# Sliding-window attention with a leaky-ReLU feed-forward behind it: first layer by halves of 288 tokens, rings for its operands, attention steps placed by matmul time, output tiles copied and issued by ACT

## Chip, cores, metric

One core of one Trainium2 chip. The metric is the time of one launch on the device in microseconds, median of several runs. Engines: PE does matmuls, DVE and ACT elementwise work (both reach the matmul result banks), POOL elementwise work in SBUF, SP only issues transfers.

## The reference

```python
# q, k, v: 8 batches x 8 heads x 576 tokens x 64, float32; window 32
scores = (q @ k.T) / 8;  mask = abs(i - j) <= 32
attn = softmax(where(mask, scores, -1e9));  y = attn @ v
x = y.transpose(0, 2, 1, 3).reshape(4608, 512)
h = x @ w_in                      # 512 -> 2048
g = maximum(0.01 * h, h)
out = g @ w_out                   # 2048 -> 512, float32
```

## The kernel before

The attention of one half batch (288 queries) and one pair of heads is a *step*; four steps make the 288 tokens of a half ready, 64 steps are done in all. A step is: `score` of the next step (five matmuls into `ps`, `exp` on ACT into `e`, mask on POOL into `pr`) and `weighted` of this one:

```python
def weighted(i):
    ...
    x = xps.tile([128, HALF], FP32, name="x")      # one bank each
    s = xps.tile([128, HALF], FP32, name="s")
    nc.tensor.matmul(s, ones_bd, pr[:, 0:HALF], ...)          # 2 matmuls: row sums
    ...                                                       # 5 matmuls into x
    r = attn.tile([128, HALF], FP32, name="r")
    nc.vector.reciprocal(r, s)
    t0 = b * S + hf * HALF
    nc.vector.tensor_mul(xT[:, p, t0:t0 + HALF], x, r)
```

The feed-forward works in groups of 256 or 384 tokens. `h_tile` makes 128 rows of the first layer in one of three banks (`mm`), and ACT empties it; `o_tile` makes 128 tokens of output in one of the same three banks:

```python
def h_tile(t0, n, f):
    h = mmps.tile([128, 512], FP32, name="mm", tag="mm")
    for c in range(DMC):                                      # 4 matmuls of n columns
        nc.tensor.matmul(h[:, 0:n], w_in_bf[:, c, ts(f, 128)], xT[:, c, ds(t0, n)], ...)
    nc.scalar.activation(out=gT[t0][:, f, 0:n], in_=h[:, 0:n], func=AF.Prelu, alpha=0.01)

def o_tile(t0, j, midway=None):
    o = mmps.tile([128, 512], FP32, name="mm", tag="mm")
    for f in range(FFC):                                      # 16 matmuls of 512 columns
        nc.tensor.matmul(o, gT[t0][:, f, ts(j, 128)], w_out_bf[:, f, :], ...)
        ...
    o_sb = outp.tile([128, DMODEL], FP32, name="o_sb")
    nc.vector.tensor_copy(out=o_sb, in_=o)
    nc.sync.dma_start(out=out[ds(t0 + j * 128, 128), :], in_=o_sb)
```

Transposes of q and k (`tp`, one bank, emptied by ACT into `qT` and `kT`; DVE copies `kT` into `kbd`) come one group of six with most steps. Where the steps stand is decided by pieces (a third or half of a group's first layer, or one output tile), not by time:

```python
groups = [(512 + 256 * i, 256) for i in range(3)]
groups += [(1280 + 384 * i, 384) for i in range(8)] + [(1280 + 384 * 8, 256)]
...                                                           # groups -> pieces ("chunks")
for ci, (_, kind, t0, n, a, m) in enumerate(chunks):
    goal = base + -(-(NC - base) * (ci + 1) // span)
    for cj in range(ci, len(chunks)):
        lead = 1 if cj < 12 else 2
        goal = max(goal, chunks[cj][0] - int(RATE * max(cj - lead - ci, 0)))
    while state["done"] < min(goal, NC):
        step()                                                # one, two or none
    ...
```

A group of 384 tokens does not match halves of 288: some groups need one new half, others two.

The softmax here doesn't subtract the row's maximum and nothing guards it: scores larger than these inputs give would overflow.

## Time and profile before

| | busy, us | share |
|---|---|---|
| PE matmul | 324.3 | 92% |
| DVE | 211.8 | 60% |
| ACT | 183.4 | 52% |
| POOL | 178.7 | 51% |
| span of the profiled run | 353.9 | |
| time, median | 356.09 | |

PE is busy nearly all the time, so the question is where it is not. The view of what PE waited for tells who held it, but its times are shorter than the loss, since a matmul's record runs on for about 0.17 us after the next could have started. To size a loss, the prediction and this document take the distance between the starts of two matmuls and subtract the distance usual for that pair.

What PE waited for between 50 and 320 us, kernel before, the three longest lines of five (engine, line, releaser: us in total, times, longest):

```profile
PE s L238 <- DVE r L252: 3.8, 5, 1.2
PE tp L187 <- ACT qT L195: 2.2, 3, 0.7
PE x L246 <- POOL vbd L175: 1.0, 2, 0.6
```

The first two are attention steps and transposes that stood too close behind another; the third is a step that came before POOL had cast its v (`vbd`).

### The profile page before, as it was taken

The numbers are of one execution on the slowest core, as the hardware profiler recorded it, in microseconds if no ns is written. First come the engines' busy times: TensorE is split into PE (matmuls) and PEld (weight loads), VectorE is DVE, ScalarE is ACT, GpSimd is POOL, SyncE is SP. The second block draws the span as 40 slices with busy tenths as digits, with TensorE's granted clock in tenths as the row PEclk, the third lists the DMA queues.
The fourth block names the chain that finished last, engine by engine and source line by source line (L and its number), as shares of the span: only waits on it lengthen the run. The fifth ranks groups of instructions, "written<-read, shape, count | busy, mean of one in ns | idle before, by whom it ended". The sixth has DMA issues, their size and how long they took to land.

```text
span 353.9 us, 6635 instructions
## 1 busy us (share of the span) xinstructions
PE 324.3 (92%) x2600; PEld 208.2 (59%) x2624; DVE 211.8 (60%) x242; ACT 183.4 (52%) x363; POOL 178.7 (51%) x213
## 2 busy tenths in 40 slices
PE   2658998999989898999999898999999999999995
PEld 1437864584957655656656555656656656555472
DVE  5588647757686877645653778554676676630101
ACT  5765862292845637518527527716528517326060
POOL 7797676578765766524543568533655423200000
PEclk9999999999999999999999999999999999999999
DMA  8999986599995274342453265340010010020101
GB/s 187 214 205 236 269 162 182 144 201 235 209 255 146 58 222 133 69 126 88 140 162 70 63 177 165 88 124 33 0 61 30 2 61 31 5 86 0 61 31 59
DMA packets 60707, 42.37 MB, mean 120 GB/s; under 512 B 39684, under 2 KB 56068, under 8 KB 60676
## 3 DMA queue, kind: packets, MB, share of 16 engines
q1 hardware_dynamic: 56388, 37.76, 42.7%
q0 software_dynamic: 4288, 4.20, 7.2%
q8 instruction: 20, 0.33, 0.4%
q14 instruction: 11, 0.09, 0.1%
HBM read 36.70 MB, written 9.44 MB: 130 GB/s over the span
## 4 chain that ended last, share of the span: by engine, by line
PE 77%; DMA 7%; DVE 6%; POOL 4%; SPq 2%; issue 2%; ACT 1%; DVEq 0%; POOLq 0%; ACTq 0%
PE mm L273 33%; PE mm L264 31%; DMA kf<-in_k_dram 7%; DVE r L252 5%; PE x L246 3%; PE tp L187 3%; PE ps L220 3%; PE s L238 2%; PE s L239 2%; SPq L71 1%; POOL vbd L175 1%; POOL vbd L400 1%; SPq L82 1%; DVE xT L254 1%; POOL pr L230 1%
## 5 line engine op out<-in xcount | busy, mean ns | idle before, releaser
L252 DVE RECIPROCAL r<-s 128x288 f32<-128x288 f32 x64 | 125.1, 1954 | 38.5 <-PE s L239 38.2
L230 POOL TENSOR_TENSOR pr<-e,mask 128x544 bf16<-128x544 bf16 x64 | 77.7, 1213 | 115.0 <-ACT e L226 114.7
L264 PE MATMUL mm<-xT,w_in_bf 128*128 128x384 bf16 (+1 forms) x896 | 132.7, 304 | 0.9 <-ACT kT L201 0.8
L268 ACT ACTIVATE gT<-mm 128x384 bf16<-128x384 f32 (+1 forms) x224 | 99.0, 445 | 63.0 <-PE mm L264 58.6
L273 PE MATMUL mm<-w_out_bf,gT 128*128 128x512 bf16 x552 | 126.8, 379 | 1.3
L264 PEld LDWEIGHTS <-w_in_bf 128*128 128x128 bf16 x896 | 86.6, 98 | 38.0 <-issue 1.3
L273 PEld LDWEIGHTS <-gT 128*128 128x128 bf16 x576 | 54.9, 98 | 61.1
L226 ACT ACTIVATE e<-ps 128x544 bf16<-128x544 f32 x64 | 39.8, 622 | 77.6 <-PE ps L220 77.6
L280 DVE COPY o_sb<-mm 128x512 f32<-128x512 f32 x36 | 24.9, 691 | 66.8 <-PE mm L273 66.8
L204 DVE COPY kbd<-kT 64x576 bf16<-64x576 bf16 x64 | 28.4, 444 | 18.2 <-ACT kT L201 17.6
L175 POOL CAST vbd<-vf 64x576 bf16<-64x576 f32 x58 | 38.3, 661 | 1.9
L254 DVE TENSOR_TENSOR xT<-x,r 128x288 bf16<-128x288 f32 x64 | 29.3, 458 | 7.0 <-PE mm L264 0.5
L165 POOL CAST kb<-kf 96x768 bf16<-96x768 f32 x32 | 26.6, 834 | 9.5 <-DMA kf<-in_k_dram 9.5
L246 PE MATMUL x<-pr,vbd 128*128 128x128 bf16 (+2 forms) x320 | 26.9, 217 | 2.0 <-POOL vbd L175 1.0
L220 PE MATMUL ps<-qT,kbd 128*128 128x128 bf16 (+2 forms) x320 | 27.3, 219 | 0.3
L238 PE MATMUL s<-pr,ones_bd 128*128 128x288 bf16 x64 | 19.0, 297 | 8.7 <-DVE r L252 7.0
L220 PEld LDWEIGHTS <-kbd 128*128 128x128 bf16 x320 | 21.1, 102 | 8.1 <-issue 0.6
L195 ACT ACTIVATE qT<-tp 128x576 bf16<-128x576 bf16 x32 | 20.8, 649 | 9.6 <-PE tp L187 9.0
L246 PEld LDWEIGHTS <-vbd 128*128 128x128 bf16 x320 | 21.4, 101 | 7.1 <-issue 2.8
L201 ACT ACTIVATE kT<-tp 128x576 bf16<-128x576 bf16 x32 | 20.8, 650 | 8.9 <-PE tp L187 7.9
L187 PE MATMUL tp<-ident,qb 96*128 96x96 bf16 x192 | 14.4, 214 | 8.5 <-DVE qb L165 6.7
L165 POOL CAST qb<-qf 96x768 bf16<-96x768 f32 x24 | 19.7, 820 | 0.0
(31 smaller groups left out, 107.7 us busy)
## 6 DMA issues: line engine op xcount, KB each, us to landing
qf<-in_q_dram SPq DMA_DIRECT2D x32, 288.0 KB, 3.5
kf<-in_k_dram SPq DMA_DIRECT2D x32, 288.0 KB, 3.9
vf<-in_v_dram SPq DMA_DIRECT2D x64, 144.0 KB, 3.4
out_dram<-o_sb SPq DMA_DIRECT2D x36, 256.0 KB, 2.2
w_in_bf<-in_moe_w_in_dram POOLq DMA_DIRECT2D x8, 256.0 KB, 6.4
w_out_bf<-in_moe_w_out_dram POOLq DMA_DIRECT2D x4, 512.0 KB, 13.5
qf<-w_in_bf SPq DMA_DIRECT2D x1, 0.0 KB
vf<-w_out_bf SPq DMA_DIRECT2D x1, 0.0 KB
```

The costliest lines, as they stand in the source:

```text
L165: eng.tensor_copy(out=dst[:, p], in_=src[b, p].rearrange("p a (c d) -> p c a d", d=D),)
L175: nc.gpsimd.tensor_copy(out=vbd[b % 2][r, p, :, r], in_=vf[b, p][r])
L204: nc.vector.tensor_copy(out=kbd[b % 2][r, p, :, r], in_=kT[r].rearrange("p (n j) -> p n j", j=64),)
L220: nc.tensor.matmul(ps[:, c0:c0 + n], kbd[b % 2][:, p, blk], qT[b][:, p, q0:q0 + n], start=True, stop=True,)
L226: nc.scalar.activation(out=e, in_=ps[:, 512 - HALF:512 - HALF + NCOL], func=AF.Exp, scale=scale,)
L230: nc.gpsimd.tensor_mul(pr, e, mask[hf])
L246: nc.tensor.matmul(x[:, a:a + n], vbd[b % 2][:, p, blk, :], pr[:, c0:c0 + n], start=(n_ == 0), stop=(n_ == len(WIN[hf]) - 1), skip_group_c ...
L252: nc.vector.reciprocal(r, s)
L254: nc.vector.tensor_mul(xT[:, p, t0:t0 + HALF], x, r)
L264: nc.tensor.matmul(h[:, 0:n], w_in_bf[:, c, ts(f, 128)], xT[:, c, ds(t0, n)], start=(c == 0), stop=(c == DMC - 1),)
L268: nc.scalar.activation(out=gT[t0][:, f, 0:n], in_=h[:, 0:n], func=AF.Prelu, alpha=0.01)
L273: nc.tensor.matmul(o, gT[t0][:, f, ts(j, 128)], w_out_bf[:, f, :], start=(f == 0), stop=(f == FFC - 1),)
```

## The change

The intent, read from the diff: make the unit of the feed-forward the same 288 tokens that attention delivers, so that each unit needs just four steps; hold only four such units of `xT` and `gT`; space the steps evenly by the PE time of what stands between; and take the output tiles off DVE, whose reciprocal PE waited for. Cut to its core:

```diff
-    outp = ctx.enter_context(tc.tile_pool(name="outp", bufs=2))
+    outp = ctx.enter_context(tc.tile_pool(name="outp", bufs=4))
-    xT = const.tile([128, NPAIR, NTOK], BF16)
+    RING = 4 * HALF
+    xT = const.tile([128, NPAIR, RING], BF16)
+    gT = const.tile([128, FFC, RING], BF16)
-    def h_tile(t0, n, f):
+    def h_tile(g, f):
+        t0 = g * HALF % RING
 ...                                        # n columns -> HALF (288) columns
         for f in range(FFC):
+            if hook and f % 4 == 0:
+                hook()
 ...
-        nc.vector.tensor_copy(out=o_sb, in_=o)
-        nc.sync.dma_start(out=out[ds(t0 + j * 128, 128), :], in_=o_sb)
+        nc.scalar.activation(out=o_sb, in_=o, func=AF.Copy)
+        nc.scalar.dma_start(out=out[ts(j, 128), :], in_=o_sb)
 ...                                        # after the first 576 tokens of the first layer:
+    for p in range(NPAIR):
+        load_qk(2, p)                      # was: one after each of the first output tiles
+    H_US, O_US, LEAD = 4 * (HALF / 2400 + 2.5e-3), 4 * 0.216, 4.0
 ...                                        # plan: h_tiles of half g, then the o_tiles it allows
+    for i in range(8, NC):
+        prev = 0.9 * O_US * 4 if i < 12 else at[i // 4 - 1] - LEAD
+        due.append(prev + (at[i // 4] - LEAD + (1.2 if i < 12 else 0) - prev) * (i % 4 + 1) / 4)
+    def spend(us):
+        while due and due[0] <= clock:
+            due.pop(0)
 ...
+            step()
+        clock += us
-    groups = ...; chunks = ...; RATE = 1.3; ...
```

More of the change, by code (lines that the diff above doesn't have):

```diff
@@ L50 @@
     attn = ctx.enter_context(tc.tile_pool(name="attn", bufs=2))
-    moe = ctx.enter_context(tc.tile_pool(name="moe", bufs=2))
-    outp = ctx.enter_context(tc.tile_pool(name="outp", bufs=2))
+    outp = ctx.enter_context(tc.tile_pool(name="outp", bufs=4))
     PS = bass.MemoryType.PSUM
@@ L252, in weighted @@
         nc.vector.reciprocal(r, s)
-        t0 = b * S + hf * HALF
+        t0 = (b * S + hf * HALF) % RING
         nc.vector.tensor_mul(xT[:, p, t0:t0 + HALF], x, r)
-    gT = {}
-    def h_tile(t0, n, f):
-        if f == 0:
-            gT[t0] = moe.tile([128, FFC, 512], BF16, name="gT")
+    gT = const.tile([128, FFC, RING], BF16)
+    def h_tile(g, f):
+        t0 = g * HALF % RING
         h = mmps.tile([128, 512], FP32, name="mm", tag="mm")
@@ L264, in h_tile, with o_tile @@
             nc.tensor.matmul(
-                h[:, 0:n], w_in_bf[:, c, ts(f, 128)], xT[:, c, ds(t0, n)],
+                h[:, 0:HALF], w_in_bf[:, c, ts(f, 128)], xT[:, c, ds(t0, HALF)],
                 start=(c == 0), stop=(c == DMC - 1),
             )
-        nc.scalar.activation(out=gT[t0][:, f, 0:n], in_=h[:, 0:n], func=AF.Prelu, alpha=0.01)
-    def o_tile(t0, j, midway=None):
+        nc.scalar.activation(
+            out=gT[:, f, ds(t0, HALF)], in_=h[:, 0:HALF], func=AF.Prelu, alpha=0.01,
+        )
+    def o_tile(j, hook=None):
         o = mmps.tile([128, 512], FP32, name="mm", tag="mm")
         for f in range(FFC):
+            if hook and f % 4 == 0:
+                hook()
             nc.tensor.matmul(
-                o, gT[t0][:, f, ts(j, 128)], w_out_bf[:, f, :],
+                o, gT[:, f, ds(128 * j % RING, 128)], w_out_bf[:, f, :],
                 start=(f == 0), stop=(f == FFC - 1),
             )
-            if midway and f == FFC // 2 - 1:
-                midway()
         o_sb = outp.tile([128, DMODEL], FP32, name="o_sb")
-        nc.vector.tensor_copy(out=o_sb, in_=o)
-        nc.sync.dma_start(out=out[ds(t0 + j * 128, 128), :], in_=o_sb)
+        nc.scalar.activation(out=o_sb, in_=o, func=AF.Copy)
+        nc.scalar.dma_start(out=out[ts(j, 128), :], in_=o_sb)
     NC = 2 * NPAIR * B
@@ L384 @@
     for f in range(FFC):
-        h_tile(0, 256, f)
+        h_tile(0, f)
         if f in (2, 6, 10):
@@ L395 @@
     for f in range(FFC):
-        h_tile(256, 256, f)
+        h_tile(1, f)
         if f % 4 == 3:
@@ L403 @@
     for p in range(NPAIR):
-        if p < 3:
-            cast_v(1, p)
-            if p == 2:
-                cast_v(1, 3)
-            o_tile(256 * (p // 2), p % 2, step if p == 2 else None)
-            step()
-        else:
-            o_tile(256, 1)
-        load_qk(2, p)
-    for p in range(NPAIR):
-        load_v(2, p)
-    groups = [(512 + 256 * i, 256) for i in range(3)]
-    groups += [(1280 + 384 * i, 384) for i in range(8)] + [(1280 + 384 * 8, 256)]
-    chunks = []
-    for g, (t0, n) in enumerate(groups):
-        need = 4 * -(-(t0 + n) // HALF)
-        nj = n // 128
-        for j in range(nj):
-            f = FFC * j // nj
-            chunks.append((need, "h", t0, n, f, FFC * (j + 1) // nj - f))
-        for j in range(nj):
-            chunks.append((need, "o", t0, n, j, 1))
@@ L429 @@
-    RATE = 1.3
-    base = state["done"]
-    span = len(chunks) - 10
-    for ci, (_, kind, t0, n, a, m) in enumerate(chunks):
-        goal = base + -(-(NC - base) * (ci + 1) // span)
-        for cj in range(ci, len(chunks)):
-            lead = 1 if cj < 12 else 2
-            goal = max(goal, chunks[cj][0] - int(RATE * max(cj - lead - ci, 0)))
-        while state["done"] < min(goal, NC):
-            step()
+        load_qk(2, p)
+    H_US, O_US, LEAD = 4 * (HALF / 2400 + 2.5e-3), 4 * 0.216, 4.0
@@ new lines @@
+    plan = []
+    tiles = 0
+    for g in range(1, 2 * B):
+        if g > 1:
+            plan += [(H_US, "h", g, f) for f in range(FFC)]
+        while 128 * (tiles + 1) <= HALF * (g + 1):
+            plan += [(O_US, "o", tiles, i) for i in range(4)]
+            tiles += 1
+    at, t = {}, 0.0
+    for us, kind, g, f in plan:
+        if kind == "h" and f == 0:
+            at[g] = t
+        t += us
+    due = []
+    for i in range(8, NC):
+        prev = 0.9 * O_US * 4 if i < 12 else at[i // 4 - 1] - LEAD
+        due.append(prev + (at[i // 4] - LEAD + (1.2 if i < 12 else 0) - prev) * (i % 4 + 1) / 4)
@@ L439 @@
+    clock = 0.0
+    cast_v(1, 0)
+    load_v(2, 0)
+    def spend(us):
+        nonlocal clock
+        while due and due[0] <= clock:
+            due.pop(0)
+            i = state["done"]
+            if i < 11:
+                cast_v(1, i - 7)
+                load_v(2, i - 7)
+            step()
+        clock += us
+    for us, kind, g, f in plan:
         if kind == "h":
-            for f in range(a, a + m):
-                h_tile(t0, n, f)
-        else:
-            o_tile(t0, a)
+            spend(us)
+            h_tile(g, f)
+        elif f == 0:
+            o_tile(g, lambda: spend(O_US))
```

## The prediction

> **What bounds the kernel now.** I read the page first (shares, slices, groups), then the waits of PE by stretch, then the timeline of PE, then the timelines of ACT and of the DMA queue around the places where PE stood still.
>
> ```profile
> PE 324.3 (92%) x2600; PEld 208.2 (59%) x2624; DVE 211.8 (60%) x242; ACT 183.4 (52%) x363; POOL 178.7 (51%) x213
> PE   2658998999989898999999898999999999999995
> ...
> L252 DVE RECIPROCAL r<-s 128x288 f32<-128x288 f32 x64 | 125.1, 1954 | 38.5 <-PE s L239 38.2
> ...
> L280 DVE COPY o_sb<-mm 128x512 f32<-128x512 f32 x36 | 24.9, 691 | 66.8 <-PE mm L273 66.8
> ...
> L254 DVE TENSOR_TENSOR xT<-x,r 128x288 bf16<-128x288 f32 x64 | 29.3, 458 | 7.0 <-PE mm L264 0.5
> ```
>
> PE bounds the kernel from about 28 us to 350 us: its digits are 8 or 9 there, no other engine passes 60%. So only two things can gain time: less PE work, or fewer places where PE stands still. The first 28 us (loads, first transposes, first attention steps) are not touched by the diff. The timeline shows where PE stands still:
>
> ```profile
> 101.98 0.29 PE L238 MATMUL s<-pr,ones_bd 128*128 128x288 bf16 x1
> 102.10 0.27 PE L239 MATMUL s<-pr,ones_bd 128*128 128x256 bf16 x1
> 102.21 0.40 PE L246 MATMUL x<-pr,vbd 128*128 128x96 bf16 x5
> 102.45 0.42 PE L187 MATMUL tp<-ident,qb 96*128 96x96 bf16 x6
> 102.91 0.40 PE L220 MATMUL ps<-qT,kbd 128*128 128x64 bf16 x5
> 104.55 0.30 PE L238 MATMUL s<-pr,ones_bd 128*128 128x288 bf16 x1 [1.24 <-DVE r L252]
> ...
> 118.99 0.42 PE L187 MATMUL tp<-ident,qb 96*128 96x96 bf16 x6
> 120.15 0.41 PE L187 MATMUL tp<-ident,kb 96*128 96x96 bf16 x6 [0.74 <-ACT qT L195]
> ```
>
> An attention step (ps, s, x) takes 0.71 us of PE (ps to s 0.24, s to x 0.23, x 0.24) and a transpose group 0.25. At 102 us two steps stand side by side. The second needs the bank of s, which DVE frees only after the reciprocal; so PE loses 1.40 us (ps to s took 1.64, not 0.24), and another 0.32 at x. DVE began that reciprocal late, because it was copying out an output tile, as the chain in order of time says:
>
> ```profile
> 99.96 1.96 PE mm L273 x9
> 101.92 0.02 issue
> 101.94 0.69 DVE o_sb L280
> 102.63 1.88 DVE r L252
> ```
>
> At 119 us two transpose groups stand side by side and the second waits for ACT to empty the one bank: 0.90 us.
>
> I went through the distances from one matmul's start to the next after 28 us, and set aside those of exactly one matmul more, which are records missing from the trace (24 of L273 are missing, 552 of 576). Lost time, over the usual distance: about 3.3 us from 28 to 50, 2.0 from 50 to 70, 1.5 from 70 to 100, 9.3 from 100 to 300, none later; 16 in all. Of the 9.3, four double steps or late steps (102, 135, 202, 216) and two double transposes (119, 200) make nearly all.
>
> **What the Trainium skill says.** "TensorE: Matmul & The Clock Gate", section "Wait — 56ns, not 53.3ns?": warm matmuls follow each other every N ÷ 2.4 GHz plus about 2.5 ns. The trace agrees: 20 matmuls of 384 columns from 158.01 to 161.26, 162.5 ns each (160 + 2.5); 32 of 256 columns in 3.49 us, 109 ns (106.7 + 2.5). "ScalarE: Activation LUTs", section "What ACT_TABLE_LOAD costs": an ACTIVATE with immediate operands takes 186 ns + 0.833 per column, and two in a row overlap by 93. The trace agrees within 20 ns: 490 for 384 columns (506), 384 for 256 (399); at 161.47 a gT of 0.49 was followed at 161.85. "DMA: Bandwidth & Descriptors", section "Issuing engines are not separate DMA queues": issuing from another engine changes only whose sequencer spends the issue time. The trace has that time for SP alone, not for ACT:
>
> ```profile
> L281 SPq DMA_DIRECT2D out_dram<-o_sb x36: 332/362/869, 54.1 to 350.8; - x36
> ```
>
> **The change, part by part.**
>
> *Size of the feed-forward pieces.* The first layer goes from 384 matmuls of 256 columns and 512 of 384 to 1024 of 288. Work: before 384 × 0.109 + 512 × 0.1625 = 125.1 us; after 1024 × 0.1225 = 125.4. So +0.3. The second layer (576 × 0.216 = 124.4) and attention are the same. ACT goes from 224 gT (99.0 us) to 256 of about 411 ns (interpolated between 384 and 490): 105 us.
>
> *Rings.* Only memory: four halves of xT and gT. A slot is rewritten when its readers are three halves, some 60 us, past. I expect no wait from it.
>
> *Even steps.* The instruction order of the changed kernel shows no two steps side by side any more; between two steps stand at least 12 second-layer matmuls (2.6 us) or 28 first-layer ones (3.4), apart from two gaps of 8 (1.7) near 60 us. The step needs DVE for 1.95 + 0.46 = 2.4 us, with the kbd copies (2 × 0.44) 3.3 at most, so s and x come free in time. Double transposes stand once (after a piece of 8 first-layer matmuls, near 88 us), as before. So the 9.3 us from 100 to 300 should go.
>
> *28 to 50 us.* Two waits for DVE (0.32, 0.24) go, since 16 matmuls take 1.96 us in place of 1.75. The last load of k for the second batch lands at 46.7 whatever PE does (PE lost 0.9 there); the larger pieces put 128 × 13.5 ns = 1.7 us more work ahead of it. Most of that is absorbed: gain about 1.5 us. *50 to 70 us.* The first step now comes after 24 second-layer matmuls (5.2 us) in place of 16, which is when POOL has the casts of v ready (52.7 to 55.4): gain 1.6 of 2.0.
>
> *Output tiles from ACT.* DVE is rid of 36 × 0.69 = 25 us. ACT gets 36 copies of 128x512; 490 + 128 × 0.83 = about 597 ns: 21 us; and 36 issues of about 0.36 us, with the hand-over about 0.45: 16 us. In sum ACT goes to about 183 + 6 + 21 = 210 us busy, plus 16 of issuing: 64% of the time, no bound on the whole. Locally it is one. The order "16 second-layer matmuls, step, transpose, 28 first-layer matmuls" occurs 8 times with a transpose. Take the end of the 16 as 0. ACT sees the bank 0.21 later (158.01 to 158.22 in DVE's case), copies until 0.81, issues until about 1.27, then e (0.53 to the next), then qT or kT (0.56), and starts the first gT at 2.37, done at 2.78. PE has finished step and transpose at 0.96 and fills its three banks, one of them that of the output tile, by 2.43. The fourth piece wants the bank of the first gT: PE waits about 0.45. Eight times: 3.6 us. From 70 to 100 us, where a transpose stands close to another, qT now comes after the copy and the issue: two waits grow by 0.8 and 0.5, so this stretch is worse by 1.3.
>
> *End.* The last copy takes 0.60 in place of 0.69, the landing about 2 us as before: −0.1.
>
> Sum: 356.2 − 1.5 − 1.6 + 1.3 − 9.3 + 3.6 + 0.3 − 0.1 = **348.9**, so 349.
>
> **Rivals.** *(a) ACT becomes the bound at every turn from one layer to the other.* For it: issues on SP took up to 0.87 us, and a load of v 3.3 us at 88.6, when the queue was full. If issues on ACT took 0.9 rather than 0.36, each of the 8 waits would be 1.0 us and those with only a step before 28 first-layer matmuls would come in: 8 us in place of 3.6, and about 354. Also, an issue on ACT waits for an earlier transfer that used the same semaphore, often a load on SP; by the order it lies some three steps (13 us) back, but near 57 us it is a load of k that lands only about then. Against it: after 125 us the DMA digits are 2 to 4 and most issues took 0.36. *(b) ACT is not felt at all*, since three banks and 20% slack in the first layer (0.33 against 0.49 us) swallow it. For it: the wait I find is only 0.45. Then 345. *(c) The early stage is bound by transfers and POOL anyway* and gives nothing back: all loads of q and k for the third batch are now issued at once and compete with v. Then the 3.1 us of gain before 70 us fall away: 352. For it: DMA digits of 9 around 45 us, 230 GB/s; against it: those loads queue behind v on one issuer.
>
> **Range and chances.** The limits come from adding rivals: (b) alone 345, (a) alone 354, both of the smaller doubts about ±2. I take 345.5 to 353.5. The line for 2% lies at 349.1, at my point, so chances are even: faster 0.50, within 2% 0.48, slower 0.02 (it would need ACT stalls of over 1 us at all 36 tiles).
>
> **What would show it.** Right: in the PE waits after 100 us no s waiting for r and no kb transpose waiting for qT; the first layer at 1024 matmuls; ACT near 210 us, DVE near 187; a new wait of PE mm for ACT gT, 0.3 to 0.5 us each, about 8 times. Wrong: waits of first-layer matmuls for gT of over 1 us, ACT issues over 0.6 us, s waiting for pr from POOL (e held up on ACT behind an issue), or losses of over 3 us between 50 and 100 us.

## The result

| | before | after |
|---|---|---|
| time, median (4 runs each) | 356.09 us | 350.93 us (350.80 to 351.50) |
| ratio, 95% interval | | 0.9852 (0.9830 to 0.9874) |
| span of the profiled run | 353.9 | 349.3 |
| PE, DVE, ACT, POOL busy | 324.3, 211.8, 183.4, 178.7 | 324.9, 189.2, 203.8, 179.1 |

A ratio here and below is the mean time of one kernel's fast runs over that of the other's fast runs of the same rounds, so not quite the ratio of the medians quoted. The gain is 1.5%: clear of noise, under 2%.

Page of the changed kernel, shares and groups (as in the prediction's first fence: line, engine, operation, shapes, count, then busy us, mean ns, idle before and its releaser):

```profile
PE 324.9 (93%) x2731; PEld 221.3 (63%) x2752; DVE 189.2 (54%) x206; ACT 203.8 (58%) x431; POOL 179.1 (51%) x213
...
L266 PE MATMUL mm<-xT,w_in_bf 128*128 128x288 bf16 x1024 | 136.8, 288 | 1.5 <-ACT gT L270 1.5
...
L270 ACT ACTIVATE gT<-mm 128x288 bf16<-128x288 f32 x256 | 101.9, 413 | 23.0 <-PE mm L266 8.8
...
L285 ACT ACTIVATE o_sb<-mm 128x512 f32<-128x512 f32 x36 | 21.5, 597 | 85.6 <-PE mm L280 85.6
```

What PE waited for between 50 and 320 us, changed kernel, the whole list:

```profile
PE tp L188 <- ACT qT L196: 1.9, 2, 1.1
PE mm L266 <- ACT gT L270: 1.5, 8, 0.2
```

`s` no longer waits for the reciprocal, as expected. A new line has come, and it is the one the prediction named: first-layer matmuls wait for ACT, eight times. One of the eight, on PE (an L266 piece, a wait of 0.18 after the modelled end; start to start the loss is 0.35 us):

```profile
114.42 0.42 PE L188 MATMUL tp<-ident,kb 96*128 96x96 bf16 x6
114.68 1.64 PE L266 MATMUL mm<-xT,w_in_bf 128*128 128x288 bf16 x12
116.50 2.12 PE L266 MATMUL mm<-xT,w_in_bf 128*128 128x288 bf16 x16 [0.18 <-ACT gT L270]
```

The same place on ACT (start, duration; ACTq is the sequencer, which issues the transfer while the engine stands still):

```profile
113.91 0.60 ACT L285 ACTIVATE o_sb<-mm 128x512 f32<-128x512 f32 x1 [2.19 <-PE mm L280]
114.54 0.34 ACTq L286 DMA_DIRECT2D out_dram<-o_sb  x1
114.98 0.62 ACT L227 ACTIVATE e<-ps 128x544 bf16<-128x544 f32 x1 [0.47 <-PE tp L188]
115.50 0.65 ACT L202 ACTIVATE kT<-tp 128x576 bf16<-128x576 bf16 x1
116.03 3.04 ACT L270 ACTIVATE gT<-mm 128x288 bf16<-128x288 f32 x7
```

Twelve matmuls fill the three banks from 114.68 on. The first bank was ready for ACT at about 115.38 (0.49 for four matmuls, 0.21 until ACT sees it), but ACT came to it at 116.03, behind copy, issue, `e` and `kT`. The line blames "tp" for the 0.47 before `e`; the transposes of that step had long been issued, and what fills the gap is the issue between 114.51 and 114.98: 0.03 to notice that the copy is done, 0.34, and 0.10 to the next instruction.

So the predicted mechanism is in the trace, and the time is still 2.0 us longer than predicted. Lost time by stretch, from the start-to-start distances (the last column is a second trace of the same kernel, the experiment `again` below):

| stretch | before | after, predicted | after, measured | taken again |
|---|---|---|---|---|
| first layer's start (about 28 us) to first output tile | 3.3 | 1.8 | 3.6 | 2.5 |
| first output tile to 70 us | 2.0 | 0.4 | 0.6 | 2.0 |
| 70 to 100 us | 1.5 | 2.8 | 2.8 | 2.8 |
| 100 to 300 us | 9.3 | 3.6 | 3.5 | 3.5 |
| after 300 us | 0 | 0 | 0.3 | 0.3 |

The missing 2 us lie before 70 us: in this trace nearly all of them before the first output tile, where the first layer also began 0.6 us later than in the trace of before (28.91 against 28.27). The experiments were chosen to find their cause, and to price each part of the change by itself.

### The profile page after: what moved, and what is told of

Read it like the earlier page. It is cut to its first block, busy times and chain, and to the rows that moved or that the text cites. A ratio compares the mean times of both kernels' runs of the same rounds, so it can differ in the third digit from the quotient of the medians.

```text
span 349.3 us, 6917 instructions
## 1 busy us (share of the span) xinstructions
PE 324.9 (93%) x2731; PEld 221.3 (63%) x2752; DVE 189.2 (54%) x206; ACT 203.8 (58%) x431; POOL 179.1 (51%) x213
## 4 chain that ended last, share of the span: by engine, by line
PE 82%; ACT 5%; DVE 3%; issue 2%; DMA 2%; SPq 2%; POOL 1%; ACTq 1%; DVEq 0%; POOLq 0%
PE mm L280 35%; PE mm L266 33%; PE x L247 4%; PE tp L188 3%; PE ps L221 3%; DVE r L253 2%; DMA kf<-in_k_dram 2%; PE s L239 2%; ACT o_sb L285 2%; PE s L240 2%; ACT gT L270 1%; SPq L81 1%; SPq L70 1%; ACTq L286 1%; ACT kT L202 1%
## 5 line engine op out<-in xcount | busy, mean ns | idle before, releaser
L266 PE MATMUL mm<-xT,w_in_bf 128*128 128x288 bf16 x1024 | 136.8, 288 | 1.5 <-ACT gT L270 1.5
L280 PE MATMUL mm<-w_out_bf,gT 128*128 128x512 bf16 x555 | 128.1, 379 | 1.1
L266 PEld LDWEIGHTS <-w_in_bf 128*128 128x128 bf16 x1024 | 98.8, 98 | 28.7 <-issue 3.2
L270 ACT ACTIVATE gT<-mm 128x288 bf16<-128x288 f32 x256 | 101.9, 413 | 23.0 <-PE mm L266 8.8
L285 ACT ACTIVATE o_sb<-mm 128x512 f32<-128x512 f32 x36 | 21.5, 597 | 85.6 <-PE mm L280 85.6
```

Of the source, the lines that this page charges most:

```text
L266: nc.tensor.matmul(h[:, 0:HALF], w_in_bf[:, c, ts(f, 128)], xT[:, c, ds(t0, HALF)], start=(c == 0), stop=(c == DMC - 1),)
L270: nc.scalar.activation(out=gT[:, f, ds(t0, HALF)], in_=h[:, 0:HALF], func=AF.Prelu, alpha=0.01,)
L280: nc.tensor.matmul(o, gT[:, f, ds(128 * j % RING, 128)], w_out_bf[:, f, :], start=(f == 0), stop=(f == FFC - 1),)
L285: nc.scalar.activation(out=o_sb, in_=o, func=AF.Copy)
```

## Experiments

Theories before them: (T1) evenly placed steps give the gain, and ACT's issue gives part of it back; (T2) DVE was what held PE, and the move of the tiles to ACT gives the gain; (T3) for the missing 2 us: the clock of PE rose at 33.8 us in the changed kernel's trace and at 30.1 in that of before, which either belongs to the change or is chance; or something holds the stretch from 50 to 70 us.

In the traces of the changed kernel and its variants I took the start of fixed matmuls: first output tile (o0), first matmul of the first layer of halves 2, 4, 6 and 15, and the last matmul. The matmuls between two such marks are the same in all of these, so the distances can be compared directly (us; worked out from the traces' start times):

| run | o0 at | half 2 at | o0 to 2 | 2 to 4 | 4 to 6 | 6 to 15 | 15 to last |
|---|---|---|---|---|---|---|---|
| the changed kernel | 52.25 | 70.20 | 17.96 | 44.48 | 38.18 | 174.11 | 18.19 |
| again | 51.03 | 70.41 | 19.38 | 44.48 | 38.18 | 174.11 | 18.19 |
| warm | 50.24 | 70.36 | 20.13 | 44.48 | 38.18 | 174.13 | 18.19 |
| late_qk | 51.23 | 68.95 | 17.72 | 44.47 | 38.18 | 174.11 | 18.19 |
| tp_mm | 51.42 | 70.26 | 18.84 | 42.27 | 38.18 | 174.12 | 18.18 |
| issue_sp | 51.39 | 69.11 | 17.72 | 43.55 | 37.26 | 171.51 | 17.98 |
| out_dve | 50.68 | 68.40 | 17.72 | 43.31 | 37.24 | 171.48 | 17.98 |
| sp_tp | 51.11 | 68.83 | 17.72 | 41.78 | 37.26 | 171.51 | 17.98 |
| dve_tp | 51.31 | 69.03 | 17.72 | 41.78 | 37.24 | 171.48 | 17.98 |
| dve_tp_warm | 50.29 | 68.01 | 17.72 | 41.78 | 37.25 | 171.48 | 17.98 |

### again: the changed kernel, unedited

> The changed kernel once more, for its trace. Theory: the 2.0 us by which the prediction was too fast lie before the first output tile (first 28 us 0.6 us later, full clock reached at 33.8 us in place of 30.1). If that belongs to the change, the first output tile starts again at about 52.2 us and the clock rises again at about 33.8. Rival: it is chance of where the clock rises; then the clock rises elsewhere, near 30, the first output tile starts about 50.5 and the time is about 349.5.

One look: 351.2 us. The clock rose at 31.4 us, o0 came at 51.03, 1.2 us earlier than in the first trace, and half 2 began at 70.41, no earlier. So where the clock rises is not a property of the change, and it does not set the time: something else lets half 2 begin at about 70.3. Both theories in the expectation fall, the second because the earlier start gained nothing. The chain that ended last in this run, from 52 to 70 us, in order of time:

```profile
53.84 7.49 DMA kf<-in_k_dram
...
61.40 0.34 ACTq L286
...
61.84 0.63 ACT e L227
...
62.61 1.22 POOL pr L231
...
63.87 0.28 PE s L239
```

ACT had finished copying the second output tile at 59.44, but did not issue it until 61.40. The chain says what it waited for: a load of k, issued on SP at 53.84 and landed at 61.32. The transfer of the tile has nothing to do with that load. The instruction order, which lists the semaphores, has it: the program gives its transfers eight semaphores in turn, whether SP or ACT issues them, and an issue waits until the earlier transfer on its semaphore has landed. On ACT such a wait delays `e`, then `pr`, then the step, and PE lost 2.0 us between 61 and 67 us.

The first trace has the same wait, but a shorter one, since PE came to it 1.2 us later:

```profile
60.06 0.60 ACT L285 ACTIVATE o_sb<-mm 128x512 f32<-128x512 f32 x1 [1.51 <-PE mm L280]
61.20 0.34 ACTq L286 DMA_DIRECT2D out_dram<-o_sb  x1
```

The copy ended at 60.66, the load of k landed at 61.12, the issue began at 61.20, and PE lost only 0.6 us from 50 to 70 us. The traces name the semaphore of each transfer: in both, load and issue have the same one (105). In all five traces with these loads and issues in these places (these two, warm, tp_mm, old_rule) the issue began 0.07 to 0.08 us after that load had landed. So the two losses take turns: an earlier start is lost again in the wait.

### issue_sp and out_dve: the output part undone, by half and whole

```diff
 # issue_sp                                              # out_dve
-    nc.scalar.dma_start(out=out[...], in_=o_sb)         -    nc.scalar.activation(out=o_sb, in_=o, func=AF.Copy)
+    nc.sync.dma_start(out=out[...], in_=o_sb)           +    nc.vector.tensor_copy(out=o_sb, in_=o)
                                                         -    nc.scalar.dma_start(...)
                                                         +    nc.sync.dma_start(...)
```

> The output tiles are copied by ACT as in the changed kernel, but their transfers are issued by SP as before. Theory: the 8 waits of 0.35 us at the start of a first-layer half come from the issue on ACT (0.34 us and the hand-over, together 0.45); without it they go, 2.8 us, and the two waits near 85 and 91 us shrink by about 0.5 and 0.4: 347.3 us. Rival: the copy on ACT alone makes them, or SP has the tiles wait behind its loads: 350 to 351.

> Output tiles copied by DVE and issued by SP, as in the kernel before; the rest is the changed kernel. Theory (mine): with evenly spaced steps DVE has the time (2.4 to 3.3 us of work for a step, 0.69 for a tile, at least 4.4 us between steps after 70 us), so moving the tiles to ACT gains nothing and costs the 8 waits of 0.35: 347 to 348 us. Rival (what the change seems to intend): copies on DVE delay the reciprocal, s comes free too late, and PE waits: 352 or more.

Measured: issue_sp 344.91 us, ratio to before 0.9682 (0.9661 to 0.9703); out_dve 344.79 us, 0.9686 (0.9664 to 0.9708). Both are some 6 us faster than the changed kernel and faster than I expected. What PE waited for between 50 and 320 us in out_dve, the whole list, and then PE at the place that answers to 114.42 above:

```profile
PE tp L188 <- ACT qT L196: 0.8, 1, 0.8
PE x L247 <- DVE xT L255: 0.2, 1, 0.2
```

```profile
111.45 0.42 PE L188 MATMUL tp<-ident,kb 96*128 96x96 bf16 x6
111.71 3.60 PE L266 MATMUL mm<-xT,w_in_bf 128*128 128x288 bf16 x28
115.14 0.40 PE L221 MATMUL ps<-qT,kbd 128*128 128x64 bf16 x5
```

28 matmuls in 3.43 us, 122.5 ns each: no gap. That issue_sp and out_dve are alike says that the *copy* costs the same on either engine, and that the whole price is the *issue* on ACT. By the table, issue_sp against the changed kernel taken again: 1.66 from o0 to half 2, 0.93 from 2 to 4, 0.92 from 4 to 6, 2.60 from 6 to 15, 0.21 at the end, 6.3 in all; 6.0 by the medians. T2 falls: with the steps spaced and the tiles on DVE, PE loses nothing after 100 us.

### before_even: the kernel before, with only the placing of the steps changed

Groups of 256 and 384, whole `xT`, tiles on DVE and SP all stay. The loop over pieces is replaced by due times, as even as the groups' needs allow:

```diff
+        ends.append((t - LEAD, 4 * -(-(t0 + n) // HALF)))   # when, and how many steps, for each group
 ...
+    while n0 < NC:
+        rate, end, upto = max(((m - n0) / (e - at), e, m) for e, m in ends if m > n0)
+        due += [at + (i + 1) / rate for i in range(upto - n0)]
+        at, n0 = end, upto
```

> The kernel before (groups of 256 and 384 tokens, whole xT, output tiles on DVE and SP) with the steps spaced evenly by PE time between the times at which a group needs them. No two steps stand side by side. Theory: the waits from 100 to 300 us (9.3 us) came from the placing alone and most of them go without halves, rings or ACT: 348 to 350. Rival: the halves or the move to ACT are needed: 353 or more.

Measured: 348.69 us, ratio 0.9790 (0.9767 to 0.9814): 7 us of gain by placing alone, more than the whole change brought. T1 holds. Against out_dve it lacks 4 us. I ran nothing that splits those, but the two traces, by the start-to-start distances, account for 3 of them. The largest part is the start, which this variant has from the kernel before: between 53 and 65 us PE lost 2.0 us on POOL's casts of v and masks, where out_dve lost 0.3. From 70 to 100 us it lost 0.3 more than out_dve, from 100 to 300 us 1.0 more.

### before_out_act: the kernel before, with only the output tiles moved to ACT

```diff
-    nc.vector.tensor_copy(out=o_sb, in_=o)
-    nc.sync.dma_start(out=out[...], in_=o_sb)
+    nc.scalar.activation(out=o_sb, in_=o, func=AF.Copy)
+    nc.scalar.dma_start(out=out[...], in_=o_sb)
```

> The kernel before with the output tiles copied and issued by ACT (four fewer microseconds of nothing else changed). Theory: the double steps stay, so two of the four places lose 0.7 us less each (those where DVE was copying a tile), and little else moves: 354.5 to 356. Rival: DVE was what held the kernel before, and most of the gain is here: 352 or less.

Measured: 361.34 us, ratio 1.0139 (1.0111 to 1.0168), 5.6 us *slower*; both theories in the expectation were wrong. (The words on "four fewer microseconds" there are a slip; the edit is the four lines above.) ACT between 59 and 62 us:

```profile
59.59 0.60 ACT L280 ACTIVATE o_sb<-mm 128x512 f32<-128x512 f32 x1 [2.74 <-PE mm L273]
61.53 0.34 ACTq L281 DMA_DIRECT2D out_dram<-o_sb  x1
61.98 0.62 ACT L226 ACTIVATE e<-ps 128x544 bf16<-128x544 f32 x1 [1.79 <-DMA qf<-in_q_dram]
```

The same wait as in `again`, this time for a load of q. PE stood still for long there, and then its clock fell for a while, which the windows of this run show (busy us and counts of PE, PEld, DVE, ACT, POOL, then granted clock, DMA share, GB/s):

```profile
60.00:64.00 4.00, 2.39 (x19) 1.16 (x17) 2.42 (x2) 1.43 (x3) 1.26 (x2) 1.00 1.07 307
64.00:68.00 4.00, 3.06 (x13) 1.39 (x13) 2.42 (x2) 0.00 (x0) 3.74 (x5) 0.60 1.20 222
```

Against the trace of before, the stretch from first output tile to the next first-layer group took 22.1 us in place of 19.4, and the one after it 22.0 in place of 20.3, where a transpose waited 1.66 and another 0.95 for ACT; elsewhere the DVE time saved and the ACT time spent nearly balance. The clock is not what makes this variant slower: the record has a granted clock of 0.995 for the profiled run and one other, but of 0.999 and 1.000 for the remaining two, and these took 360.56 and 361.73 us.

### old_rule: the changed kernel with steps placed by the old rule

The `due` times of halves 2 to 15 are replaced by the loop over pieces of the kernel before, with pieces made from halves.

> The changed kernel with the steps placed by the rule of the kernel before (thirds or halves of a first-layer group and whole output tiles as pieces, counted by pieces and not by PE time). By the instruction order four steps still fall into each half and none stand side by side. Theory: it is the halves that even the steps out, since each half of 288 tokens needs just four; the placing by time adds little: 350.5 to 352. Rival: the exact spacing by time is what gains: 354 or more.

Measured: 352.20 us (350.91 to 354.44), ratio 0.9896 (0.9851 to 0.9942). The median lies 0.2 us above the range of the theory and well under the rival's 354, with more scatter (the slowest run has a granted clock of 0.994). So, once the units are halves, the old rule already spaces the steps nearly well enough: in the trace PE lost 1.1 us more from 70 to 100 us than in the changed kernel, and no more after that. That exact due times gain this 1 us in time is not shown, as the two intervals overlap. Halves without due times (old_rule) and due times without halves (before_even) are two ways to the same end.

### late_qk: the loads that ACT waited for, issued later

```diff
-    for p in range(NPAIR):
-        load_qk(2, p)
 ...
             step()
+            if i < 12:
+                load_qk(2, i - 8)
```

> The changed kernel with the loads of q and k for the third batch issued one pair after each of the steps 8 to 11, and not all at once before the first output tile. Theory: in the changed kernel ACT's second issue waits until 61.4 us for a load of k (issued at 53.84, landed 61.32) that used the same semaphore, and e and the steps behind it are late; that costs about 1.7 us at 61 to 66 us and swallows any earlier start. With the loads later the issue waits for nothing that is still on its way: 349.3 us, no issue on ACT more than 0.1 us after its copy before 70 us. Rival: the stretch is held by POOL and the loads of v, and the later loads of q and k come too late for the casts: 351 or more.

Measured: 350.14 us, ratio 0.9837 (0.9816 to 0.9858). In the trace the second issue comes 0.03 us after its copy, and o0 to half 2 takes 17.72 us, exactly as with no issue on ACT: that ACT waited for those loads, and what it cost there, is shown. Half 2 begins at 68.95, 1.25 to 1.5 us earlier than in the two traces of the changed kernel. The time fell by 0.8 us against the first timing of the changed kernel, half of what I expected, and the two intervals overlap.

### warm: useless matmuls that raise the clock earlier

```diff
+    def warm():
 ...
+        d = mmps.tile([128, 512], FP32, name="mm", tag="mm")
+        for _ in range(2):
+            nc.tensor.matmul(d, ident, mask[0][:, 0:512], start=True, stop=True)
 ...
+        if i > 0:
+            warm()
         weighted(i)                        # steps 1 to 3
```

> The changed kernel with two useless matmuls of 512 columns ahead of the second, third and fourth attention step, where PE waits about 1.1 us for s. Theory: [...]with PE kept busy from 20 to 28 us it is at full rate when the first layer starts, and the first-layer matmuls take 122 ns in place of 240 from the start: 1.7 us less, 349.2. Rival: the clock does not depend on these waits, or the useless matmuls delay the steps: 351 to 352.

Measured: 351.36 us, ratio 0.9866 (0.9848 to 0.9884). The clock rose at 25.7 us, and o0 came at 50.24, the earliest of all, but half 2 began at 70.36 as ever: PE waited longer for the steps held up by ACT's issue. The useless matmuls did move the clock's rise: to 25.7 us here and 23.2 in dve_tp_warm, where the twelve traces without them have 30.1 to 34.1. The expectation failed because the stretch behind was held by something else. (Two of its four runs have a granted clock of 0.995, 351.58 and 351.73 us; the other two, at 1.000, took 351.14 and 350.65, so they show no gain either.)

### tp_mm: the third batch's transposes in the three feed-forward banks

```diff
-                t_parts[b] = transposes(b)
+                t_parts[b] = transposes(b, first=b == 2)
```

> The changed kernel with the transposes of the third batch (70 to 95 us) in the three feed-forward banks in place of the single transpose bank. Theory: the four waits of kb for qT there (0.23, 0.24, 0.95, 1.28 us) come from the one bank; they go, though first-layer pieces may wait a little for banks: 2.0 us less, 349.0. Rival: ACT is what is late there, and first-layer matmuls wait for it in place of the transposes: 350.5 to 351.

Measured: 348.67 us, ratio 0.9792 (0.9771 to 0.9814); half 2 to 4 fell from 44.48 to 42.27 us. The waits of `kb` for `qT` came from the single bank.

### sp_tp, dve_tp, dve_tp_warm: the parts that gained, together

issue_sp with the edit of tp_mm; out_dve with it; and that with the edit of warm.

> Copies of the output tiles on ACT, issues on SP, and the transposes of the third batch in the feed-forward banks. Theory: the two changes are at different places and add: 344.9 less 1.8 (0.23, 0.23, 0.42, 0.95 at 73 to 90 us) is 343.1. Rival: with the transposes no longer waiting, first-layer pieces wait for ACT: 344 to 345.

> Output tiles on DVE and SP, and the transposes of the third batch in the feed-forward banks. Theory: 344.8 less 1.6 is 343.2, the same as with copies on ACT, since neither engine is short of time. Rival as for the other.

> The one with tiles on DVE and transposes in the feed-forward banks, and with the useless matmuls that raise the PE clock before the first layer. Theory: on the changed kernel they gained nothing because ACT's second issue waited for a load whatever PE did; with no issue on ACT the earlier start stays, as far as the last load of k lets it (0.7 us were lost to it at 47.6 us): 0.3 to 1.0 us less than without, 342.5. Rival: the loads hold the first 60 us anyway: the same time.

Measured: 343.29 us (ratio 0.9642), 343.40 us (0.9646) and 342.26 us (0.9612, 0.9590 to 0.9633). The first two are as expected and alike. With no issue on ACT the earlier clock now reaches the end: half 2 begins at 68.01 in place of 69.03, and the time is 1.1 us less (the intervals of the two just overlap). The last of the three beats both kernels, by 3.9% and by 2.4%. Its trace has two waits of PE left between 40 and 320 us, 0.4 us for `kT` (the last load of k) and 0.2 for `xT`.

## Why the prediction was right, and where it was not

By its range it was right: 350.93 lies between 345.5 and 353.5, and within 2% of before was given 0.48. The point was 2.0 us too low. The terms after 70 us came out within 0.3 us; the two before it did not.

- *PE bounds, and stands still where steps stand side by side.* Right. Placing alone gained 7 us (before_even), and after 50 us no `s` waits for `r` any more.
- *First layer +0.3, rings without waits.* Right: 122.5 ns a matmul, and no wait of the lists is for a ring's slot.
- *100 to 300 us: −9.3 and +3.6.* Right in the sum (3.5 us lost in place of 3.6), slightly wrong in the parts: eight waits of 0.35 for ACT, 2.8 us and not 3.6, and three waits of 0.25 of `x` for `xT`, which I had not counted. Copy and issue took what was predicted (`e` began 1.27 us after the 16 matmuls); `e` and `kT` took 0.05 less, and PE had the bank 0.06 after `gT` in place of the 0.10 that the sum implies. The waits for `xT` go with the issue (issue_sp, out_dve), because `kT`, and with it `kbd` ahead of the reciprocal on DVE, was late on ACT too.
- *70 to 100 us: +1.3.* Right: 2.8 us lost in place of 1.5.
- *28 to 50 us: gain 1.5.* **Too large.** From the first layer's start to o0, PE lost 3.3 us in the trace of before (the half clock before its rise included), and 3.6 and 3.5 in those of before_even and before_out_act, which are the same program up to there; with halves it lost 2.2 to 3.6, median 2.6, in the nine traces without useless matmuls. So the gain is some 0.7 to 1.0, and in the first trace of the changed kernel there was none. Part of the scatter is where the clock rises. The prediction also took the 0.9 us lost to the last load of k for a fixed cost; of the three traces with the old start only the one it read has it.
- *50 to 70 us: gain 1.6 of 2.0.* **This step failed as a term to be added to the one before.** In the first trace it came out (0.6 lost in place of 0.4), but there o0 was late; taken again, o0 was earlier and PE lost 2.0. With ACT's issue behind the load of k, half 2 began at 70.2 to 70.4 in four traces whose o0 lay between 50.24 and 52.25. The two terms put it at 67.7 (49.70 + 1.73 of added work − 1.5, then 17.4 of work and 0.4 lost). late_qk takes this wait away and gives back 0.8 us by the medians, 1.25 to 1.5 by the marks; the rest of the miss is the term from 28 to 50 us. The prediction had the mechanism, a load of k "that lands only about then" on the same semaphore, as a clause of its first rival, and left it out of the sum.
- *Rival (c), the early stage gives nothing back: 352.* Nearer to the time than the sum was, but for another reason: the loads held PE through ACT's issue. With the issue on SP and the same loads, half 2 begins at 68.4 to 69.1 (issue_sp, out_dve, sp_tp, dve_tp).
- *"ACT 4.8 in sum"* (3.6 + 1.3 − 0.1): it is 6.0 to 6.3, by the medians and the table of marks. The difference is the wait of the step from 50 to 70 us.
- *Signs of being wrong.* Two of them came: PE lost 3.4 us between 50 and 100 us (4.8 taken again), where the limit was "over 3", though the prediction's own terms there, 0.4 and 2.8, already make 3.2; and taken again, `s` waited 1.0 us for `pr` behind an `e` held up on ACT. In rival (b), 0.33 against 0.49 us is a slack of 33%, not 20%.

The reading that an average of 58% makes ACT no bound was correct and of no use: what counts is that ACT's sequencer takes issues and activations in one order.

## What to carry to other kernels

Place work that has a fixed minimum distance (here 2.4 us of DVE between two steps) by time and not by pieces; matching the sizes of producer and consumer does most of that by itself. Do not let an engine that the critical engine waits for issue transfers: besides its 0.47 us each, an issue can stand behind any transfer that used its semaphore before, and the engine stands with it. Before counting on an earlier start, look for the event behind it that does not move; an improvement ahead of it (warm) shows only once that is gone (dve_tp_warm).

## What the Trainium skill lacked or had wrong

- "DMA: Bandwidth & Descriptors", section "Issuing engines are not separate DMA queues", treats the issuing engine as a matter of sequencer time that "is usually small". It lacks what the time costs on an engine that also computes: 36 issues on ACT, 0.34 us each and 0.47 with both hand-overs, made the kernel 6.0 us longer than the same issues on SP (350.93 against 344.91), and one of them held ACT for 1.96 us (59.44 to 61.40) behind another engine's load.
- "ScalarE: Activation LUTs", section "What ACT_TABLE_LOAD costs": 186 ns + 0.833 per column is 13 to 16 ns more than measured (413 ns for 288 columns, page 426; 597 for 512, page 612). Two activations of 288 columns that both wait start 0.29 to 0.32 us apart, an overlap of 0.09 to 0.12, where the page has about 0.093.
- "TensorE: Matmul & The Clock Gate", section "What's actually happening", has the clock fall after at least one idle window of about 3.4 us. In before_out_act it stood at half from 64.8 to 68.2 us, although by the matmul records PE was busy for 1.38 of the 3.41 us before the fall; in warm, PE was busy for 1.80 of the 3.41 us from 60.55 on, and it did not fall. Where the line lies between, or what else decides, the runs do not show; the same section says only that recent activity decides.
